# Attention with routed experts on one core: fills moved from GpSimd to VectorE, routing of two batches spread over three pairs, output transposes moved beside the products with v

## The chip, the cores and the metric

The kernel runs on one core of one Trainium2 chip. The metric is the device time of one execution in microseconds, median over the runs; lower is better. PE is TensorE (matmuls, transposes), DVE VectorE, ACT ScalarE, POOL GpSimd, SP the engine that issues most DMAs.

## The reference, cut to what matters

Inputs: q, k, v of 4 batches x 8 heads x 768 tokens x 64 values in float32, and 16 centroids per head. Every query and every key goes to the nearest centroid of its head; a query attends only to keys of its own cluster.

```python
q_assign = np.argmax(np.einsum('bhsd,hcd->bhsc', q_n, c_n), axis=-1)
k_assign = np.argmax(np.einsum('bhsd,hcd->bhsc', k_n, c_n), axis=-1)
scores = np.where(q_assign[..., None] == k_assign[..., None, :], scale * q @ k.T, -1e9)
attn = softmax(scores);  x = attn @ v                     # 3072 tokens x 512
do_compute = x @ w_skip > 0
e_idx = np.argmax(x @ w_gate, axis=1)                     # 1 of 8 experts per token
out = x;  out[do_compute] += gate_w * (relu(x @ w1[e]) @ w2[e])
```

## The kernel before, in words

**Pairs and steps.** The 32 heads are worked through as 16 pairs of heads, four pairs to a batch. A pair has 24 score steps (`score`, L654): two fp32r matmuls, L660 and L661, make a 128 x 384 tile of scores in a PSUM bank (high parts, mask rows and row maxima in L660, the low parts in L661), ACT takes the exponential (L663), GpSimd adds the tiles of a half up for the softmax sums (L669, L675). Beside the scores of one pair PE makes the row maxima of the next (`smax`, L601), each reduced by DVE (L603); L614 joins the maxima of a half, and `max_rows` (L620, L623, L628), or `mrows` (L635, L640) in pairs 0 and 1, turns them into rows of the query operand. Twice a pair, near steps 7.7 and 19.7, PE does the 12 or 24 products with v (`avs`, L686) of the half before. In the same places stand the transposes of the clusters (`assign`, L546, followed on DVE by `first_max` L526 to L539), the masks (L559), the softmax sums (L722, L734) and the output transposes (`xout`, L785, scaled by ACT in L807).

**Routing.** When the four pairs of a batch have been through, the batch is routed to the experts. `route_a` (L852) makes the logits; `route_gates` chooses the expert (L927, L934, L945) and computes the gate (`gate`: L954, L956, then g in L960, L962, L964, and its split in three bf16 parts L968 and L971, and L945 again); `route_slots` computes each token's slot: `route_c` (PE L981 to L984, DVE L988, L992, L996, L999, the one-hot rows L1003 in two pieces, L1007), `route_cum` (L1033, L1035) and `route_d` (DVE L1017 twice, PE L1022, DVE L1026). Nothing of this is wanted before the last batch is through. Then the experts run (`experts`) on the tokens that the slots list.

**Order.** A table of due times, counted in score steps, sets the order of everything up to the experts. A task of pair i with time t is due at step 24i + t; `steps` (L324) takes tasks from a heap by their due time, and every engine gets its instructions in that order. A generator yields either a delay or, in a tuple, a new due time from the start of its pair: the tables `GATES` and `SLOTS` are such times for the routing, counted from the start of the batch's last pair. So 67.66 in batch 0 (last pair 3) is step 19.66 of pair 5, and 79.66 is step 7.66 of pair 6.

**Banks.** Seven PSUM banks go round: `take` (L409) hands out the one that has been free longest, `give` (L418) puts it back. A matmul that needs a bank waits until the reader of seven takes ago has finished, so a DVE that lags stops PE. The eighth bank belongs to the products with v.

**The start.** Before pair 0 GpSimd fills operand tiles by memsets: `wraw` (L308), the two tiles MC that take the joined maxima (L312) and two rows of the query operands of pairs 1 and 2 (L315); then it does half of the low parts of pair 0 (`lo_first`, L495) and those of pair 1 (`split_lo`, L463), and `zero_rows` (L437) clears the mask rows.

Of the kernel before, what the change touches and what calls it, by code (L numbers as in the profile page):

```python
# [13 lines left out]
F32 = mybir.dt.float32  # L14
# [11 lines left out]
HP = H // 2  # L26
# [21 lines left out]
    "sims": -52.25, "assign": (-40.58, 0.23, 0.01, 0.01, 0.01, 0.01),  # L48
    "hi": (-40.33, -40.3), "masks": (-28.6, 0.12), "lo": (-28.35, -28.3), "copies": (-23.3, -23.2, -23.1),
    "smax": (-21.1, 1.0, -0.4), "mneg": (-9.0, 3.2), "mrows": ((-4.57, 0.1, 0.05), (7.4, 0.1, 0.05)),  # L50
    "av": (7.6, 13.6, 19.6), "oT": (3.5, 3.55), "sums": 43.73, "recip": 55.38, "xout": (67.43, 79.42, 37.55),
    "route": (36.0, 43.3, 58.9), "early": (85.4, 100.9),
}
OWN = {"sums": 29.2, "recip": 31.5, "xout": (31.52, 49.55, 37.55)}
ROWS = {"mrows": ((-4.5, 0.2, 0.05), (5.5, 0.1, 0.05))}

GATES = (43.31, 43.32, 43.64, 43.65, 43.66, 55.66, 55.67, 55.68, 55.69, 55.7, 55.71, 56.5,
         67.66, 67.67, 67.68, 67.69, 67.7, 67.71, 67.72, 67.73, 67.74)
SLOTS = (59.1, 60.6, 61.6, 62.6, 72.6, 74.6, 77.16, 77.17, 77.18, 77.19, 79.66, 82.9, 83.1)
FIRST = {  # L60
    0: {
        "load_v": -18.9, "sims": -20.0, "hi": (-19.9, -19.8, -19.7, -19.6), "assign": (-19.0, 0.1, 0.01, 0.01, 0.01, 0.01),
# [26 lines left out]
class Kernel:  # L89
# [202 lines left out]
    def operand_buffers(self):  # L292

        nc, fix, npair = self.nc, self.fix, self.npair
        for i in range(min(3, npair)):
            for a in range(2):
                kk = self.KB[i][a].bitcast(F32)

                lo = 64 if i else 96
                if a:  # L300
                    nc.gpsimd.memset(kk[96:98, :], 1.0)
                    nc.gpsimd.memset(kk[lo:97, :], 0.0)
                else:
                    nc.gpsimd.memset(kk[lo:98, :], 0.0)
                    nc.gpsimd.memset(kk[96:97, :], 1.0)

        self.MX = [self.mx0[:, hf * HALF:(hf + 1) * HALF].rearrange("p (b q) -> p b q", b=NB) for hf in range(2)]
        nc.gpsimd.memset(self.mx0[:, :S], 0.0)  # L308

        self.MC = [fix.tile([P, P], F32R, name=f"MC{hf}") for hf in range(2)]  # L310
        for t in self.MC:
            nc.gpsimd.memset(t.bitcast(F32), 0.0)  # L312
        for i in range(1, 3):
            for a in range(2):
                nc.gpsimd.memset(self.QM[i][a].bitcast(F32)[96:98, :], 0.0)  # L315

        self.M = [fix.tile([P, KT, 2, 3], F32, name=f"M{n}") for n in range(2)]
        for t in self.M:
            nc.vector.memset(t[:, :, :, 2:], -BIG / 2)
        nc.vector.memset(self.PT[:, :, HALF:], GUARD / S)  # L320
        for t in self.P2:
            nc.vector.memset(self.pair_of(t)[:, :, HALF:], GUARD / S)
# [24 lines left out]
    def tasks(self, i):  # L347

        p, last = dict(PLAN), i == self.npair - 1
        if not 1 < i < self.npair - 2:  # L350
            p.update(ROWS)
        if not 1 < i < self.npair - 3:
            p.update(OWN)
        elif i % HP == HP - 1:
            p["sums"], p["recip"] = 31.75, 40.0
        if i == 1:
            p["xout"] = (31.52, 55.41)
        p.update(FIRST.get(i, {}))
        r = [(s, lambda s=s: self.score(i, s)) for s in range(NS)]
        add = lambda t, f, *a: r.append((t, lambda: f(i, *a)))  # L360
        if i:
            add(p["load"], self.load)
        add(p["load_v"], self.load_v)
        if i in (1, 2):
            add(-15.0 - i * NS, self.zero_rows)
        add(p["sims"], self.sims)
        add(p["assign"][0], self.assign, *p["assign"][1:])
        if i:
            for t in range(2):
                add(p["hi"][t], self.split_hi, t)  # L370
                add(p["lo"][t], self.split_lo, t)
            add(p["copies"][0], self.copies_hi)
            for t in range(2):
                add(p["copies"][1 + t], self.copies_lo, t)
            add(p["masks"][0], self.masks, *p["masks"][1:])
        else:
            for n in range(4):
                add(p["hi"][n], self.hi_first, n % 2, n // 2)
                add(p["lo"][n], self.lo_first, n % 2, n // 2)
            add(p["masks"], self.masks_first)  # L380
        t0, dt, gap, dt2 = (*p["smax"], p["smax"][1])[:4]
        for n in range(24):
            add(t0 + dt * n if n < 12 else t0 + 12 * dt + gap + dt2 * (n - 12), self.smax, n)
        for hf in range(2):
            add(p["mneg"][hf], self.mneg, hf)
            add(p["mrows"][hf][0], self.max_rows if i > 1 else self.mrows, hf, *p["mrows"][hf][1:])
            if not 3 - hf <= i < self.npair - 2:
                for n in range(2):
                    add(12 * hf + p["av"][n], self.avs, hf, range(n * GROUP, (n + 1) * GROUP))
            else:  # L390
                add(12 * hf + p["av"][1 if hf and i == self.npair - 3 else 2], self.avs, hf, range(KT))
        if not last:
            add(p["sums"], self.sums, (0, 1))
            add(p["recip"], self.recip)
            for hf in range(2):
                add(p["xout"][2 if hf and i == self.npair - 2 else hf], self.xout, hf)
        if i == self.npair - HP - 1:
            for t, f in zip(p["early"], (self.early_lists, self.early_rows)):
                add(t, f)
        if last:  # L400
            for t, f, *a in self.ending(i):
                add(t, f, *a)
        elif i % HP == HP - 1:
            add(p["route"][0], self.route_a, i // HP)
            add(p["route"][1], self.route_gates, i // HP)
            add(p["route"][2], self.route_slots, i // HP)
        return r

    def take(self, key, shape):  # L409
# [24 lines left out]
    def zero_rows(self, i):  # L434

        for a in range(2):
            self.nc.gpsimd.memset(self.QM[i][a].bitcast(F32)[64:96, :], 0.0)  # L437

    def operands(self, i):
        c = self.st[i]  # L440
# [166 lines left out]

    def mneg(self, i, hf):

        if i:  # L610
            out = self.MC[hf][:, :2 * NB].rearrange("p (a j) -> p j a", a=2)
        else:
            out = self.MX[hf][:, :, 96:98]
        self.nc.vector.tensor_reduce(out=out, in_=self.st[i]["m"][:, hf * NB:(hf + 1) * NB], axis=AX.X, op=ALU.max)  # L614
# [247 lines left out]
    def route_gates(self, i, bt):  # L862

        nc = self.nc
        wait = iter([(t,) for t in GATES])
        lp = self.rt.tile([P, KT, H, E + 1], F32, name="lp")
        tps = []
        for hf in range(2):
            tps.append(self.take(("gs", hf), [P, NB, P]))
            for b in range(NB):  # L870
                n0 = hf * HALF + b * P
                nc.tensor.transpose(out=tps[hf][:, b, :], in_=self.rg[:, n0:n0 + P], identity=self.ident)
        for hf in range(2):
            yield next(wait)
            js = slice(hf * NB, (hf + 1) * NB)
            nc.vector.tensor_tensor(
                out=lp[:, js], in0=tps[hf].rearrange("p b (h e) -> p b h e", h=H)[:, :, :, :E + 1],
                in1=self.st[bt * HP]["rs"][:, js].unsqueeze(3).to_broadcast([P, NB, H, E + 1]), op=ALU.mult)
            self.give(("gs", hf))
        yield next(wait)  # L880
        yield from self.choose(lp, bt * KT, KT, wait)
        yield next(wait)
        yield from self.gate(i, bt * KT, KT, wait)

    def route_slots(self, i, bt):

        wait = iter([(t,) for t in SLOTS])
        yield from self.route_c(i, bt * KT, KT, wait)
        yield next(wait)
        yield from self.route_cum(KT, wait)  # L890
        yield next(wait)
        yield from self.route_d(i, bt * KT, KT, wait=wait)
# [652 lines left out]
```

## Time and profile before

| | |
|---|---|
| median of 3 runs | 655.32 us (653.06 to 657.39) |
| profiled execution | 656.28 us, of which the span of the instructions 654.4 us |
| PE busy | 630.3 us (96%) |
| DVE busy | 490.8 us (75%) |
| ACT busy | 394.6 us (60%) |
| POOL busy | 364.4 us (56%) |
| mean clock of TensorE | 0.988 of full speed |

The profiled execution is one run under the profiler; times inside it are counted in us from its first instruction. Pair 0's scores start at 20.62, pair 5 runs from 153.22 to 177.94, pair 6 to 204.60, pair 7 to 228.91, pair 9 from 256.03, pair 10 from 280.75 to 307.41; the experts begin near 436. In a row such as `[0.95 <-DVE M L603]` the bracket is the time for which the engine stood idle just before and what ended it. Matmuls overlap in the pipeline, so their starts tell more than their durations.

### The profile page before, as it was taken

What the parts mean: (1) busy time and instruction counts of PE and PEld (TensorE: products, weight loads), DVE (VectorE), ACT (ScalarE), POOL (GpSimd) and SP (SyncE); (2) the same over time, 40 slices, a digit from 0 to 9 for tenths busy, and PEclk for the clock granted to TensorE, in tenths of its full rate; (3) what the DMA queues carried; (4) which work ended last, traced back from release to release, by engine and by line L of the source; (5) the groups of instructions that cost most, each with busy time, mean ns of one, the idle gap of its engine ahead of it and who ended that gap; (6) DMA issues with size and microseconds to landing.
All of it is one profiled execution on the core that took longest, in us unless ns stands there. A gap on an engine that the chain in (4) does not pass through costs nothing.

```text
span 654.4 us, 12248 instructions
## 1 busy us (share of the span) xinstructions
PE 630.3 (96%) x3917; PEld 472.6 (72%) x3917; DVE 490.8 (75%) x1008; ACT 394.6 (60%) x907; POOL 364.4 (56%) x389
## 2 busy tenths in 40 slices
PE   7899989999999999999999999999899999999994
PEld 3576668766766777667767767646699899889783
DVE  7888587878897788988887988875869765856621
ACT  7367676666767677567766759733744645555420
POOL 9976777876778777768856867522033222211101
PEclk9799998999999999999999999999999999999998
DMA  7296666455584583674764846633386675764800
GB/s 214 78 231 161 179 166 153 145 166 131 158 221 120 146 232 97 175 179 125 202 168 132 225 108 198 210 106 113 134 261 241 209 233 195 267 204 143 275 2 33
DMA packets 54688, 110.23 MB, mean 168 GB/s; under 512 B 8783, under 2 KB 23159, under 8 KB 54624
## 3 DMA queue, kind: packets, MB, share of 16 engines
q1 hardware_dynamic: 51568, 102.01, 54.2%
q0 software_dynamic: 2656, 7.24, 3.4%
q8 instruction: 32, 0.52, 0.3%
q14 instruction: 32, 0.26, 0.1%
q10 hardware_dynamic: 400, 0.20, 0.1%
HBM read 61.00 MB, written 10.62 MB: 109 GB/s over the span
## 4 chain that ended last, share of the span: by engine, by line
PE 77%; DVE 8%; DMA 7%; issue 7%; ACT 1%; POOL 0%; SPq 0%; POOLq 0%; DVEq 0%; ACTq 0%
PE ps L686 19%; PE ps L660 10%; PE ps L601 10%; PE ps L661 9%; DVE M L603 4%; DMA out<-yo,idw 4%; PE ph L1062 3%; PE ph L1061 3%; PE ph L1060 3%; PE py L1062 2%; PE py L1060 2%; PE py L1061 2%; DMA raw<-qk 2%; PE ps L722 2%; PE ps L512 2%
## 5 line engine op out<-in xcount | busy, mean ns | idle before, releaser
L603 DVE TENSOR_REDUCE M<-ps 128x1 f32<-128x384 f32 x384 | 200.3, 554 | 60.6 <-PE ps L601 59.4
L675 POOL TENSOR_TENSOR acc<-acc,PT 128x384 f32<-128x384 f32 x134 | 126.4, 972 | 49.2 <-ACT vm L706 26.2
L660 PE MATMUL ps<-D 98*128 98x384 f32 x384 | 136.1, 355 | 1.9 <-DVE M L603 1.1
L601 PE MATMUL ps<-D 96*128 96x384 f32 x384 | 134.7, 358 | 0.8 <-ACT D L581 0.7
L675 POOL TENSOR_TENSOR acc<-acc,wraw 128x384 f32<-128x384 f32 x112 | 113.0, 1040 | 34.9 <-ACT wraw L663 34.9
L661 PE MATMUL ps<-D 128*128 128x384 f32 x384 | 131.5, 343 | 0.0
L663 ACT ACTIVATE PT<-ps 128x384 f32<-128x384 f32 x216 | 100.5, 494 | 48.5 <-PE ps L661 44.2
L663 ACT ACTIVATE wraw<-ps 128x384 f32<-128x384 f32 x168 | 81.6, 492 | 19.2 <-PE ps L661 12.6
L660 PEld LDWEIGHTS ps<-D 98*128 98x128 f32 x384 | 73.8, 192 | 20.3 <-issue 15.1
L601 PEld LDWEIGHTS ps<-D 96*128 96x128 f32 x384 | 74.3, 194 | 15.1 <-issue 6.0
L1217 POOL DMA_INDIRECT out<-yo,idw x15 | 19.3, 1287 | 116.0 <-DVE yo L1094 95.3
L686 PE MATMUL ps<-PT,vt 128*64 128x385 f32 x432 | 75.4, 492 | 0.0
L661 PEld LDWEIGHTS ps<-D 128*128 128x128 f32 x384 | 74.1, 193 | 0.0
L686 PE MATMUL ps<-wraw,vt 128*64 128x385 f32 x336 | 57.9, 492 | 0.1
L686 PEld LDWEIGHTS ps<-PT,vt 128*64 128x64 f32 x432 | 28.7, 136 | 34.8 <-issue 34.1
L1362 DVE SCALAR_TENSOR_TENSOR hl<-ph,hh 128x256 fp32r<-128x256 f32 x56 | 23.7, 423 | 38.2 <-ACT hh L1361 38.2
L1361 ACT ACTIVATE hh<-ph 128x256 fp32r<-128x256 f32 x56 | 21.5, 383 | 46.8 <-PE ph L1062 45.8
L1333 ACT ACTIVATE D<-wraw 128x1024 fp32r<-128x1024 f32 (+1 forms) x45 | 43.9, 1000 | 6.2 <-PE py L1062 6.2
L1061 PE MATMUL ph<-x2h,D 128*128 128x256 f32 x168 | 47.5, 283 | 0.0
L1060 PE MATMUL ph<-x2l,D 128*128 128x256 f32 x168 | 47.4, 283 | 0.0
L1060 PE MATMUL py<-D,hh 128*128 128x512 f32 x112 | 45.0, 402 | 0.0
L686 PEld LDWEIGHTS ps<-wraw,vt 128*64 128x64 f32 x336 | 22.7, 136 | 27.5 <-issue 26.7
(324 smaller groups left out, 1197.6 us busy)
## 6 DMA issues: line engine op xcount, KB each, us to landing
wraw<-w SPq DMA_DIRECT2D x72, 512.0 KB
D<-D SPq DMA_DIRECT2D x124, 192.0 KB
raw<-qk SPq DMA_DIRECT2D x16, 768.0 KB
D<-raw SPq DMA_DIRECT2D x60, 192.0 KB
vt<-v SPq DMA_DIRECT2D x16, 384.0 KB
out<-x SPq DMA_DIRECT2D x31, 192.0 KB
D<-mk SPq DMA_DIRECT2D x120, 24.0 KB
D<-mr SPq DMA_DIRECT2D x56, 1.5 KB
```

What stands on the lines that cost most here:

```text
L601: nc.tensor.matmul(sm, lhsT=c["qm"][a][0:96, j * P:(j + 1) * P], rhs=c["kb"][a][0:96, hf * HALF:(hf + 1) * HALF], start=True, stop=True)
L603: nc.vector.tensor_reduce(out=c["m"][:, j, a, hf:hf + 1], in_=sm, axis=AX.X, op=ALU.max)
L660: nc.tensor.matmul(ps, lhsT=c["kb"][a][0:98, ks], rhs=c["qm"][a][0:98, sl], start=True, stop=False)
L661: nc.tensor.matmul(ps, lhsT=c["kc"][a][:, ks], rhs=c["qc"][a][:, sl], start=False, stop=True)
L663: nc.scalar.activation(out=pt, in_=ps, func=AF.Exp, scale=D ** -0.5)
L675: (nc.vector if dve else nc.gpsimd).tensor_tensor(out=acc, in0=acc, in1=pt, op=ALU.add)
L686: nc.tensor.matmul(av[a * D:(a + 1) * D, :], lhsT=c["vt"][:, kt, a * D:(a + 1) * D], rhs=self.pt(i, hf * 2 * KT + kt * 2 + a), start=(kt = ...
L1060: mm(ps, lhsT=ah, rhs=bl, start=first, stop=False)
L1061: mm(ps, lhsT=ah, rhs=bh, start=False, stop=False)
L1062: mm(ps, lhsT=al, rhs=bh, start=False, stop=last)
L1333: nc.scalar.activation(out=h[:, cs], in_=r[:, cs], func=AF.Copy)
L1362: nc.vector.scalar_tensor_tensor(out=hl[:, f, :], in0=ph, scalar=0.0, in1=hh.bitcast(F32)[:, f, :], op0=ALU.max, op1=ALU.subtract)
```

## The change: fills, routing, output transposes

- **Fills.** The two memsets of MC go from GpSimd to DVE; the four of L315 go away, and `zero_rows` clears two rows more for pair 2. In pair 1 `mneg` writes the joined maxima where `mrows` reads them (`MX`); before, it wrote them to MC.
- **Routing of batches 0 and 1** (batch 2 keeps the tables; batch 3 has its own ending). The later part of the gate, from L960 on, is due at step 7.66 of pair 6 (batch 1: 10) and not at 19.66 of pair 5. The slots start at step 19.3 of pair 5 instead of 10.9, and their pieces stand at 19.66 of pair 5, 19.66 of pair 6, 7.66 and 19.3 of pair 7 (`LATE`).
- **Batch 2**: the first piece of L1003 comes from 72.6 to 67.8, the second from 74.6 to 72.6.
- **`xout`**: the output transposes of the first half from 67.43 to 67.55.

```diff
-    "av": ..., "xout": (67.43, 79.42, 37.55),
-    "route": (36.0, 43.3, 58.9), "early": (85.4, 100.9),
+    "av": ..., "xout": (67.55, 79.42, 37.55),
+    "route": (36.0, 43.3, 58.9, 67.3), "early": (85.4, 100.9),
...
-SLOTS = (59.1, 60.6, 61.6, 62.6, 72.6, 74.6, 77.16, 77.17, 77.18, 77.19, 79.66, 82.9, 83.1)
+SLOTS = (59.1, 60.6, 61.6, 62.6, 67.8, 72.6, 77.16, 77.17, 77.18, 77.19, 79.66, 82.9, 83.1)
+LATE = (79.66, 79.67, 79.68, 79.69, 79.7, 79.71, 79.72, 79.73, 79.74,
+        67.66, 67.67, 67.68, 67.69, 67.75, 91.66, 91.67, 91.68, 91.69, 103.66, 103.67, 115.3, 115.7)
...
         for t in self.MC:
-            nc.gpsimd.memset(t.bitcast(F32), 0.0)
-        for i in range(1, 3):
-            for a in range(2):
-                nc.gpsimd.memset(self.QM[i][a].bitcast(F32)[96:98, :], 0.0)
+            nc.vector.memset(t.bitcast(F32), 0.0)
...
-            add(p["route"][2], self.route_slots, i // HP)
+            add(p["route"][2 if i == self.npair - HP - 1 else 3], self.route_slots, i // HP)
...
-            self.nc.gpsimd.memset(self.QM[i][a].bitcast(F32)[64:96, :], 0.0)
+            self.nc.gpsimd.memset(self.QM[i][a].bitcast(F32)[64:96 + 2 * (i == 2), :], 0.0)
...
     def mneg(self, i, hf):
-        if i:
+        if i > 1:
             out = self.MC[hf][:, :2 * NB].rearrange("p (a j) -> p j a", a=2)
         else:
             out = self.MX[hf][:, :, 96:98]
...
     def route_gates(self, i, bt):
-        wait = iter([(t,) for t in GATES])
+        wait = iter([(t,) for t in (GATES if bt == self.nbatch - 2 else GATES[:12] + LATE[:9])])
...
     def route_slots(self, i, bt):
-        wait = iter([(t,) for t in SLOTS])
+        wait = iter([(t,) for t in (SLOTS if bt == self.nbatch - 2 else LATE[9:])])
```

From L312 on the lines of the changed kernel carry a number that is lower by one.

GpSimd's queue at the start, before (MC_205 and MC_206 are the tiles MC, D the operands):

```order
L308 MEMSET wraw 128x768
L312 MEMSET MC_205 128x128
L312 MEMSET MC_206 128x128
L315 MEMSET D 2x768 x4
L495 TENSOR_TENSOR D<-raw,D 64x768 x2
L463 TENSOR_TENSOR raw<-raw,D 128x768 x2
L437 MEMSET D 32x768 x4
L669 TENSOR_TENSOR acc<-PT 128x384 x2
```

The same place in the changed kernel:

```order
L310 MEMSET wraw 128x768
L494 TENSOR_TENSOR D<-raw,D 64x768 x2
L462 TENSOR_TENSOR raw<-raw,D 128x768 x2
L436 MEMSET D 32x768 x2
L436 MEMSET D 34x768 x2
L668 TENSOR_TENSOR acc<-PT 128x384 x2
```

Six memsets no longer stand ahead of the subtractions.

DVE's queue in pair 6, from its first row maxima to the clusters of the first products with v (M_213 and M_214 hold maxima, oht, hs, cs, cum and rhs belong to the slots of batch 0), before:

```order
L614 TENSOR_REDUCE MC_206<-M_213 128x3x2
L603 TENSOR_REDUCE M_214<-ps_88 128x1
L603 TENSOR_REDUCE M_214<-ps_91 128x1
L1007 TENSOR_TENSOR hs<-iota,hi 128x12
L1033 TENSOR_REDUCE cs<-ohd 128x8
L1035 TENSOR_TENSOR cum<-cum,cs 128x8
L1017 TENSOR_TENSOR rhs_2037<-rv,hs 128x30x8
L603 TENSOR_REDUCE M_214<-ps_89 128x1
L603 TENSOR_REDUCE M_214<-ps_94 128x1
L739 RECIPROCAL rs<-ps_92 128x3x2 x2
L526 TENSOR_REDUCE mxc<-ps_89 128x24
L1017 TENSOR_TENSOR rhs_2037<-rv,hs 128x30x8
```

The same place in the changed kernel (g and ex belong to the gate of batch 0):

```order
L602 TENSOR_REDUCE M_210<-ps_89 128x1
L602 TENSOR_REDUCE M_210<-ps_94 128x1
L602 TENSOR_REDUCE M_210<-ps_88 128x1
L602 TENSOR_REDUCE M_210<-ps_91 128x1
L738 RECIPROCAL rs<-ps_90 128x3x2 x2
L525 TENSOR_REDUCE mxc<-ps_88 128x24
L959 TENSOR_REDUCE g<-ex 128x6
L528 TENSOR_TENSOR eqc<-ps_88,mxc 128x384
L533 TENSOR_TENSOR eqc<-eqc,wts 128x384
L961 TENSOR_SCALAR g<-g 128x6
L536 TENSOR_REDUCE mwc<-eqc 128x24
L963 RECIPROCAL g<-g 128x6
```

The six pieces of the slots are gone from among the row maxima; three operations of the gate stand between the cluster operations, and six more follow them.

PE's queue at the second products of a pair (oT_103 is the attention output that is transposed), before:

```order
L785 MATMUL ps_91<-ident,oT_103 128x128 x3
L620 MATMUL ps_89<-ident_r,MC_205 128x128
L601 MATMUL ps_92<-D 128x384
L686 MATMUL ps_95<-PT,vt 64x385 x12
L512 MATMUL ps_88<-raw,cb_184 32x384 x2
```

In the changed kernel:

```order
L619 MATMUL ps_91<-ident_r,MC_205 128x128
L600 MATMUL ps_89<-D 128x384
L784 MATMUL ps_92<-ident,oT_103 128x128 x3
L685 MATMUL ps_95<-PT,vt 64x385 x12
L511 MATMUL ps_88<-raw,cb_184 32x384 x2
```

The three transposes move behind the maxima rows and one row-maximum matmul, right ahead of the products. This happens in ten pairs, 2 to 11.

## Rows read from the trace of the kernel before

**Rows 1.** Page, part 4: shares of the chain of work that ended last.

```profile
PE 77%; DVE 8%; DMA 7%; issue 7%; ACT 1%; POOL 0%; SPq 0%; POOLq 0%; DVEq 0%; ACTq 0%
```

**Rows 2.** Busy time by stretch (pairs 2, 6, 10): length, PE, PEld, DVE, ACT, POOL, clock, DMA.

```profile
75.14:102.50 27.36, 25.55 (x144) 18.65 (x145) 20.12 (x40) 18.09 (x47) 20.61 (x22) 0.95 0.58 152
...
177.94:204.60 26.66, 25.31 (x161) 17.86 (x161) 22.91 (x45) 17.79 (x47) 20.29 (x21) 1.00 0.59 156
...
280.75:307.41 26.66, 25.32 (x160) 17.87 (x160) 22.90 (x45) 17.79 (x47) 20.29 (x21) 1.00 0.59 156
```

**Rows 3.** Timeline, PE, 160 to 192: start, duration, operation, idle before.

```profile
163.29 0.34 PE L601 MATMUL ps<-D 96*128 96x384 f32 x1
...
163.46 0.34 PE L660 MATMUL ps<-D 98*128 98x384 f32 x1
...
167.22 0.33 PE L601 MATMUL ps<-D 96*128 96x384 f32 x1
...
167.81 0.44 PE L660 MATMUL ps<-D 98*128 98x384 f32 x1 [0.25 <-DVE M L603]
...
181.95 0.45 PE L660 MATMUL ps<-D 98*128 98x384 f32 x1 [0.34 <-DVE M L603]
...
183.34 0.52 PE L785 MATMUL ps<-ident,oT 128*128 128x128 f32 x3
...
184.80 0.55 PE L546 MATMUL ps<-ident,ss 128*128 128x128 f32 x3 [0.95 <-DVE M L603]
```

**Rows 4.** Timeline, DVE, 160 to 191.

```profile
166.05 0.19 DVE L992 TENSOR_REDUCE rank<-rk 128x6 f32<-128x48 f32 x1
...
166.62 0.68 DVE L996 TENSOR_SCALAR hi<-rank 128x6 f32<-128x6 f32 x1
...
171.94 0.74 DVE L962 TENSOR_SCALAR g<-g 128x6 f32<-128x6 f32 x1
...
175.10 0.31 DVE L945 TENSOR_TENSOR rv<-vals,ohd 128x144 bf16<-128x144 bf16 x1
...
176.55 2.68 DVE L603 TENSOR_REDUCE M<-ps 128x1 f32<-128x384 f32 x5 [1.14 <-PE ps L601]
...
185.86 1.20 DVE L1017 TENSOR_TENSOR rhs<-rv,hs 128x240 bf16<-128x240 bf16 x1
```

**Rows 5.** Timeline, DVE and POOL, around the first products of pair 7.

```profile
212.64 0.66 DVE L539 TENSOR_TENSOR oh<-wts,mwc 128x384 bf16<-128x384 f32 x1
...
214.33 2.15 DVE L603 TENSOR_REDUCE M<-ps 128x1 f32<-128x384 f32 x4 [1.03 <-PE ps L601]
...
215.67 3.63 POOL L675 TENSOR_TENSOR acc<-acc,PT 128x384 f32<-128x384 f32 x4 [2.78 <-ACT vm L706]
```

**Rows 6.** Timeline, POOL, at the start.

```profile
13.28 2.77 POOL L315 MEMSET D<- 2x768 f32 x4
...
19.90 3.91 POOL L463 TENSOR_TENSOR raw<-raw,D 128x768 fp32r<-128x768 f32 x2
```

**Rows 7.** Timeline, DVE and PE, at the start.

```profile
22.75 1.47 DVE L539 TENSOR_TENSOR oh<-wts,mwc 128x384 bf16<-128x384 f32 x1
...
22.63 0.52 PE L661 MATMUL ps<-D 128*128 128x384 f32 x1
...
24.28 0.50 PE L559 MATMUL ps<-ident_bf,oh 128*128 128x128 bf16 x3 [1.13 <-DVE oh L539]
```

**Rows 8.** Busy time by stretch, at the start (columns as in Rows 2).

```profile
20.00:25.00 5.00, 3.30 (x13) 2.67 (x13) 4.90 (x6) 2.52 (x6) 4.94 (x4) 0.62 0.46 162
...
25.00:30.00 5.00, 5.00 (x25) 4.06 (x25) 3.28 (x8) 2.46 (x5) 4.92 (x7) 0.70 0.11 26
```

**Rows 9.** Timeline, PE, in pair 2.

```profile
98.24 0.85 PE L512 MATMUL ps<-raw,cb 128*32 128x384 f32 x8 [1.81 <-DMA raw<-qk]
```

**Rows 10.** Timeline, PE and DVE, in pair 1.

```profile
56.63 0.49 PE L635 MATMUL ps<-ident,wraw 128*128 128x128 f32 x3
...
56.74 0.17 DVE L614 TENSOR_REDUCE MC<-M 128x6 fp32r<-128x18 f32 x1
```

More of the change, by code (lines that the diff above doesn't have):

```diff
@@ L50 @@
     "smax": (-21.1, 1.0, -0.4), "mneg": (-9.0, 3.2), "mrows": ((-4.57, 0.1, 0.05), (7.4, 0.1, 0.05)),
-    "av": (7.6, 13.6, 19.6), "oT": (3.5, 3.55), "sums": 43.73, "recip": 55.38, "xout": (67.43, 79.42, 37.55),
-    "route": (36.0, 43.3, 58.9), "early": (85.4, 100.9),
+    "av": (7.6, 13.6, 19.6), "oT": (3.5, 3.55), "sums": 43.73, "recip": 55.38, "xout": (67.55, 79.42, 37.55),
+    "route": (36.0, 43.3, 58.9, 67.3), "early": (85.4, 100.9),
 }
```

## The prediction, as put on record

> **What bounds the kernel now.** I read the chain of waits first: PE is 77% of it [rows 1]. Then the busy times pair by pair, with the pairs' first scores as limits, to see where PE is not busy. Pairs 6 and 10, the second pairs after the last of a batch, last 26.66 us each with PE busy for 25.31 and 25.32 [rows 2], so 1.35 us each is idle. Both carry the same routing steps, for batch 0 and batch 1, and show the same numbers. Everything else between the start and the experts is PE with no gap to speak of, except the start and pair 2. So I looked in PE's timeline for what ends the idle time [rows 3], in DVE's for what stood in DVE's queue there [rows 4], and at the start [rows 6 to 8]. The change does not touch the experts, about a third of the span.
>
> The stalls in pairs 5 and 6 work like this. Seven PSUM banks go round, and a lagging DVE returns the bank of a row maximum late; PE then waits for L603. At 167.81 PE waited 0.25 us, at 181.95 0.34, at 184.80 0.95 [rows 3], 1.54 in all. Each restart also costs: the first matmul behind a wait lasts 0.44 to 0.55 instead of 0.34. From start to start, L601 to L660 takes 0.17 in the ordinary case (163.29 to 163.46) and 0.59 at 167.22 to 167.81, so this stall is worth 0.42 and not 0.25. I add 0.16 to each: 0.42 + 0.50 + 1.11 = **2.0 us per batch**, 4.0 for two.
>
> How much lag is free? Ahead of 167.81, L992 (0.19), a multiply of the same size and L996 (0.68) had been put in among the maxima [rows 4], about 1.07 us; PE lost 0.42. So about **0.65 us** of lag costs PE nothing, an estimate.
>
> **The change, part by part.**
>
> *Routing out of the maxima.* The six slot pieces no longer stand among the row maxima of pairs 5 and 6; they come next to products with v, where DVE has no maxima to make. I take off the whole 2.0 per batch. The pieces and the gate need cover in their new places:
> - Pair 5, second products: L988 to L999 and a piece of L1003 take the place of the nine gate operations. Those ran from 171.94 (L962) to 175.41 (end of L945), and DVE still idled 1.14 us before the next maximum at 176.55 [rows 4]. The new ones are fewer. Cost nothing; without the cover, about as much as was taken off.
> - Pair 6, second products: the other piece of L1003 and L1007 to L1035. The same cover, not otherwise used. Nothing.
> - Pair 6, first products: the nine gate operations, behind and among the cluster operations. The cover is to be read in pair 7, which has no routing there: L539 starts at 212.64, lasts 0.66, and the next maximum comes at 214.33 after 1.03 us idle [rows 5]. Upper bound: the gate as it ran beside GpSimd's adds, 175.41 − 171.94 less one L463 that ran in between and plus L960, about 2.8 us; 2.8 − 1.03 − 0.65 = 1.1 us of stall. Lower bound: nine operations of 0.2, the price of L992 or L945 at 0.19 to 0.31, 1.9 us: 1.9 − 1.03 − 0.65 = 0.2. I take 0.25, near the lower end, because in pair 7 GpSimd has done its adds by then: it idled 2.78 us before 215.67 [rows 5], so from 212.9, and the last six operations run without it.
> - Pair 7, first products: L1017 twice. One took 1.20 beside the adds [rows 4]: 2.4 − 1.03 − 0.65 = 0.75 at most, 0 at least. I take 0.1: the gap is half filled at the least price and one of the two can be expected to be short.
>
> Left over per batch 0.35 (0 to 1.85). PE's own routing matmuls only move. **Routing: −4.0 + 0.7 = −3.3 us** (−4.0 to −0.3).
>
> *Fills.* GpSimd's four memsets of L315 take 2.77 us from 13.28 on; then come L495 and L463 (19.90, for 3.91) [rows 6]. DVE's L539 at 22.75, beside L463, took 1.47 us, against 0.66 in pair 7 [rows 5, 7]; L534 before it was held up alike. PE came to L559 after the L661 of 22.63, which is over in 0.52 with its successor due after 0.32, and started at 24.28: 1.33 us lost, 1.13 of it named as waiting for L539 [rows 7]. With 2.77 us less ahead of it, L463 ends near 21 and L539 is done before PE asks. All of the 1.33 goes. DVE's two new memsets lie in its idle time before the first clusters: nothing; without that cover, two at the price of L992, 0.4.
>
> What the 1.33 is worth depends on the clock. TensorE ran at a mean granted clock of 0.62 from 20 to 25 and 0.70 from 25 to 30, though busy throughout the second stretch [rows 8]: half of these ten us was at the lower of the two levels, 1.2 GHz, and 0.38 × 5 + 0.30 × 5 = 3.4 us of full-speed work was lost. Pair 2 shows what one spell of waiting costs: after the 1.81 us at 98.24 [rows 9] the clock of the pair is 0.95 of 27.36 us [rows 2], 1.4 lost. The start has two idle spells, before the first score and at L559. If the low clock lasts as long as now, only about 0.6 of the 1.33 is kept, 0.8. If the second spell is what prolongs it, up to half of the 3.4 is added: 0.8 + 1.7 = 2.5. I take **−1.9**, above the middle, since two spells cost over twice what one did.
>
> *Maxima of pair 1.* L635 at 56.63 now waits for L614, which starts at 56.74 and ends at 56.91 [rows 10]: **+0.3** (0 to 0.3). Behind the wait on PE stand the maxima and scores; they come that much later. In the first half L614 is done long before.
>
> *Batch 2.* One piece of L1003 moves to just ahead of maxima that follow the products without pause. Its nearest price is L1017's 1.20; less 0.65, at most 0.5. It leaves an equal lag later. **+0.2** (0 to 0.5).
>
> *Output transposes.* The same PE instructions in another order, ten times. L785's three lie between matmuls either way; a pitch may be 0.05 longer or shorter. **0** (−0.5 to +0.5). ACT's and SP's order is unchanged; the maxima rows leave PE a little sooner, for which nobody waits.
>
> **Sum:** −3.3 − 1.9 + 0.3 + 0.2 = −4.7. The profiled execution took 656.28, its span plus 1.9; that gives 651.6. It stands 1.0 above the median of the runs shown, so against the median it would be 650.6. I forecast **651.0 us**.
>
> **A rule that speaks against the new places.** Operations of the same size cost very different times here: L962 on 128 x 6 elements took 0.74, L992, which reads eight times as much, 0.19 [rows 4]. The Trainium skill ("SBUF — State Buffer", section "Who interferes with whom") says that DVE and GpSimd share a port pair, that a copy, cast or tensor_scalar in a two-port mode contends for it and that whoever came first blocks the other for its whole instruction, while a tensor_reduce never contends. By that rule a gate operation amid the adds would wait out what is left of an add. The two rows agree with it. By the rule alone all four tensor_scalar and cast operations of the gate would be long in pair 6, and the time would be that of the second rival.
>
> **Rivals.**
> 1. *The clock stays low as long as now.* The start gives 0.8 instead of 1.9: 652.1. For it: the first idle spell stays. Chance 0.2.
> 2. *The gate waits behind GpSimd's adds again.* Four operations at 0.74 and two long L1017: the left-over is 1.85 per batch and not 0.35, so 651.0 + 3.0 = 654.0. For it: rows 4; against: GpSimd idles by the end of the clusters [rows 5]. Chance 0.15.
> 3. *Slower.* The stall moves into one place, the first maximum after the gate in pairs 6 and 10, and grows to what waiting cost in pair 2. If the gate's 2.8 us meets both adds and cluster operations that are each lengthened as L539 was at the start (by 0.8), the lag is 2.8 + 0.8 − 1.03 = 2.6, the stall 1.9: that is the length that preceded a low clock at 98.24, and another 1.4 us go. Per batch 3.3 against 2.0 taken off, plus pair 7's 0.75: +2.05, so +4.1 in all, and with the start −1.9 and +0.5: 656.3 + 2.7 = 659.0. It decides from a stall of 1.8 us; rows 5 speak against. Chance 0.04.
> 4. *Better.* Nothing is left over, the start gives 2.5 and the low clock in pair 2 is spared by another timing of that wait: 651.0 − 0.7 − 0.6 − 1.4 = 648.3. Chance 0.15.
>
> That the slots come too late cannot be: L1026 of batch 1 is due in pair 11, far ahead of the experts.
>
> **How the numbers follow.** The forecast's own case has 0.46. The range **647 to 655** takes in the forecast, rivals 1, 2 and 4 and the bounds of the sum on either side but for the extremes together. 1% is 6.55 us, about what can be told from no change: 648.8 to 661.9. Faster by over 1%: rival 4 and the lower edge of the forecast, 0.17. Slower by over 1%: 0.02, the worse half of rival 3. Within: the rest, 0.81.
>
> **What would show it.** Pairs 6 and 10 should last about 25 us, with PE idle 0.5 at most; PE should no longer wait for L603 ahead of L546. L495 should start near 13.5, L559 near 23, and the clock from 25 to 30 be above 0.70. L635 in pair 1 should be released by L614. I am wrong if the gate's operations in pair 6 hold back the next row maximum by over 1.7 us, if pair 5 stalls anew, or if the start is no shorter.

## The result, and the profile after

| | before | changed |
|---|---|---|
| median | 655.09 us (653.06 to 657.39, 4 runs) | 647.89 us (647.10 to 649.57, 4 runs) |
| ratio, 95% interval | | 0.9882 (0.9861 to 0.9902) |
| profiled execution | 656.28 us, span 654.4 | 649.57 us, span 647.7 |

The change makes the kernel 1.2% faster, 7.2 us between the medians and 6.7 between the two profiled executions. The forecast was 651.0, range 647 to 655. I lay out the spans of the two profiles by pairs, from first score to first score; the columns are those of [rows 2].

| stretch | before | changed | difference |
|---|---|---|---|
| start, to the first score | 20.62 | 20.95 | +0.33 |
| pair 0 | 28.25 | 27.46 | -0.79 |
| pair 1 | 26.26 | 26.51 | +0.25 |
| pair 2 | 27.36 | 25.02 | -2.34 |
| pairs 3 and 4 | 50.72 | 50.89 | +0.17 |
| pairs 5, 6, 7 | 75.69 | 73.47 | -2.22 |
| pair 8 | 27.12 | 27.17 | +0.05 |
| pairs 9, 10, 11 | 75.69 | 73.48 | -2.21 |
| pairs 12 to 15 | 104.07 | 104.19 | +0.12 |
| experts to the end | 218.60 | 218.58 | -0.02 |

Busy time of the changed kernel in pairs 0, 2, 6 and 10:

```profile
20.95:48.41 27.46, 26.34 (x138) 20.05 (x138) 21.57 (x40) 16.35 (x35) 20.75 (x24) 0.88 0.63 150
74.91:99.93 25.02, 24.10 (x145) 17.21 (x145) 19.98 (x40) 18.13 (x47) 18.78 (x21) 1.00 0.64 167
...
174.99:199.71 24.72, 24.72 (x154) 17.92 (x154) 23.02 (x50) 17.77 (x47) 18.27 (x21) 1.00 0.62 168
...
275.64:300.37 24.73, 24.73 (x155) 17.93 (x155) 22.72 (x50) 17.76 (x47) 19.31 (x21) 1.00 0.62 167
```

The 0.33 by which the first score comes later is not the fills': in the eight other kernels with the same memsets (below) it comes at 20.62 to 20.69.

Pairs 6 and 10 are now wholly PE: length and busy time are equal, where 1.35 us was idle [rows 2]. Where PE waited 0.95 us ahead of L546 [rows 3], PE's timeline now shows

```profile
179.45 0.52 PE L784 MATMUL ps<-ident,oT 128*128 128x128 f32 x3
179.80 0.49 PE L545 MATMUL ps<-ident,ss 128*128 128x128 f32 x3
```

0.35 us from start to start instead of 1.46. DVE's timeline at the gate's new place in pair 6 and at the two L1016 in pair 7 (L1017 before):

```profile
182.32 0.97 DVE L961 TENSOR_SCALAR g<-g 128x6 f32<-128x6 f32 x1
...
183.78 0.56 DVE L538 TENSOR_TENSOR oh<-wts,mwc 128x384 bf16<-128x384 f32 x1
184.26 0.17 DVE L967 CAST vals<-g 128x6 bf16<-128x6 f32 x1
...
185.29 0.31 DVE L944 TENSOR_TENSOR rv<-vals,ohd 128x144 bf16<-128x144 bf16 x1
185.51 1.94 DVE L602 TENSOR_REDUCE M<-ps 128x1 f32<-128x384 f32 x4
...
205.52 0.64 DVE L1016 TENSOR_TENSOR rhs<-rv,hs 128x240 bf16<-128x240 bf16 x1
...
207.23 1.20 DVE L1016 TENSOR_TENSOR rhs<-rv,hs 128x240 bf16<-128x240 bf16 x1
...
209.45 2.15 DVE L602 TENSOR_REDUCE M<-ps 128x1 f32<-128x384 f32 x4
```

One gate operation among the clusters was held up (L961, 0.97); the six behind L538 took their short times, as [rows 5] let one expect once GpSimd's adds are through. The next maxima follow without idle time, so the cover of 1.03 us is used up. DVE is then late by a little more than PE can take. PE's timeline names no wait behind these products, but its starts show three delays:

```profile
186.12 0.44 PE L659 MATMUL ps<-D 98*128 98x384 f32 x1
186.40 0.34 PE L660 MATMUL ps<-D 128*128 128x384 f32 x1
...
188.17 0.34 PE L600 MATMUL ps<-D 96*128 96x384 f32 x1
188.50 0.45 PE L659 MATMUL ps<-D 98*128 98x384 f32 x1
188.78 0.34 PE L660 MATMUL ps<-D 128*128 128x384 f32 x1
```

From start to start these take 0.28, 0.33 and 0.28 us where 0.18 is usual, 0.35 in all, and all of it counts as busy. The run with the gate left where it was (below) does not have them.

At the start, POOL, DVE and PE:

```profile
13.84 3.71 POOL L494 TENSOR_TENSOR D<-raw,D 64x768 fp32r<-64x768 f32 x2 [0.93 <-DVE D L494]
17.63 3.58 POOL L462 TENSOR_TENSOR raw<-raw,D 128x768 fp32r<-128x768 f32 x2
...
22.25 0.56 DVE L538 TENSOR_TENSOR oh<-wts,mwc 128x384 bf16<-128x384 f32 x1
...
23.35 0.52 PE L660 MATMUL ps<-D 128*128 128x384 f32 x1
23.68 0.54 PE L558 MATMUL ps<-ident_bf,oh 128*128 128x128 bf16 x3
```

L462 ends at 21.2 and not at 23.8 [rows 6], L538 takes 0.56 and not 1.47 [rows 7], and L558 starts 0.33 behind the matmul ahead of it: the wait is gone. The clock is not:

```profile
20.00:25.00 5.00, 4.43 (x17) 3.88 (x17) 4.00 (x8) 2.90 (x6) 4.42 (x6) 0.58 0.18 73
25.00:30.00 5.00, 5.00 (x25) 3.99 (x25) 3.29 (x8) 2.55 (x6) 3.14 (x4) 0.74 0.13 30
```

0.42 × 5 + 0.26 × 5 = 3.4 us of full-speed work is lost, as before [rows 8]. In pair 2 the wait for the load is shorter than in [rows 9], 0.92 us, and the clock stays at 1.00:

```profile
96.93 0.85 PE L511 MATMUL ps<-raw,cb 128*32 128x384 f32 x8 [0.92 <-DMA raw<-qk]
```

In pair 1 PE waits for the maxima, but for 0.2 us only (columns: total, times, longest):

```profile
PE ps L634 <- DVE wraw L613: 0.2, 1, 0.2
```

### The profile page after: what moved, and what is told of

Same layout as the page of the kernel before. It is cut to its first block, busy times and chain, and to the rows that moved or that the text cites. A ratio compares the mean times of both kernels' runs of the same rounds, so it can differ in the third digit from the quotient of the medians.

```text
span 647.7 us, 12258 instructions
## 1 busy us (share of the span) xinstructions
PE 629.3 (97%) x3917; PEld 473.2 (73%) x3917; DVE 493.6 (76%) x1010; ACT 394.4 (61%) x907; POOL 356.0 (55%) x383
## 4 chain that ended last, share of the span: by engine, by line
PE 81%; issue 7%; DMA 6%; DVE 4%; ACT 1%; POOL 0%; POOLq 0%; SPq 0%; DVEq 0%; ACTq 0%
PE ps L685 19%; PE ps L659 11%; PE ps L600 11%; PE ps L660 10%; DMA out<-yo,idw 4%; PE ph L1060 3%; PE ph L1059 3%; PE ph L1061 3%; PE py L1061 2%; PE py L1059 2%; PE py L1060 2%; PE ps L511 2%; PE ps L721 2%; PE ps L784 2%; DVE M L602 2%
## 5 line engine op out<-in xcount | busy, mean ns | idle before, releaser
L602 DVE TENSOR_REDUCE M<-ps 128x1 f32<-128x384 f32 x384 | 199.0, 553 | 49.9 <-PE ps L600 48.6
L674 POOL TENSOR_TENSOR acc<-acc,wraw 128x384 f32<-128x384 f32 x112 | 109.1, 1006 | 38.3 <-ACT wraw L662 38.3
L662 ACT ACTIVATE wraw<-ps 128x384 f32<-128x384 f32 x168 | 81.7, 492 | 17.8 <-PE ps L660 10.9
```

The lines of the kernel that those rows point to most:

```text
L602: nc.vector.tensor_reduce(out=c["m"][:, j, a, hf:hf + 1], in_=sm, axis=AX.X, op=ALU.max)
L662: nc.scalar.activation(out=pt, in_=ps, func=AF.Exp, scale=D ** -0.5)
L674: (nc.vector if dve else nc.gpsimd).tensor_tensor(out=acc, in0=acc, in1=pt, op=ALU.add)
```

## The experiments

Each kernel was timed beside the kernel before on the same chip, and the ratios refer to that. The medians of the kernel before were 655.56 us beside the routing, the fills, the transposes and the load, 654.88 beside the dummy matmuls, the doses, the memsets and the gate, and 656.36 beside the other three.

### The parts alone

**Routing alone.** The routing's lines of the diff in the kernel before (`LATE`, the fourth entry of `route`, and the two iterators).

> The kernel before with the routing of batches 0 and 1 spread as in the change, and nothing else. Theory: the stalls behind L603 vanish without anything in their place; pairs 5 to 7 and 9 to 11 together are 2.2 us shorter per batch, 4.4 in all, ratio about 0.993; pair 0 stays at 28.2. Rival: part of the 4.4 came from an earlier start or the moved output transposes, then it is under 3.5. Pair 2: if its 2.3 us in the change came with the routing (it cannot by the order, since no routing operation stands there), it is 25.0 here, else 27.4.

650.55 us, ratio 0.9924 (0.9898 to 0.9949), that is −5.0 us (−6.7 to −3.3). Pairs 5 to 7 last 73.34 and 9 to 11 73.35 us, −4.7 together; pair 6 lasts 24.68, as in the change. Pairs 0 and 2:

```profile
20.66:47.19 26.53, 23.54 (x138) 17.27 (x138) 22.81 (x40) 16.24 (x35) 23.44 (x25) 1.00 0.69 182
73.53:100.70 27.17, 25.55 (x145) 18.64 (x145) 20.03 (x39) 17.99 (x47) 20.49 (x22) 0.95 0.59 154
...
PE ps L561 <- DVE oh L541: 1.9, 1, 1.9
```

The whole of the routing gain is here. Something else shows: pair 0, untouched by this edit, was 1.7 us shorter than in the profile before, because the clock did not fall at the start of this run, and its wait for the clusters (L561 here) was then 1.9 us long, not 1.1.

**Fills alone.** The fills' lines of the diff in the kernel before, with `mneg`.

> The kernel before with the fills alone (MC on DVE, four memsets dropped, two rows more in zero_rows, the maxima of pair 1 in MX). Theory: L559 no longer waits for L539, but TensorE's clock is as low for as long as before, so that pair 0 is 0.8 us shorter, pair 1 0.25 longer, total -0.5, ratio 0.999. Rival: the fills also shorten pair 2 by 2.3 us, because the load that it waits for comes earlier against PE; then the total is -2.9, ratio 0.9955.

652.67 us, ratio 0.9954 (0.9937 to 0.9971): −3.0 us (−4.1 to −1.9).

```profile
20.64:44.70 24.06, 23.51 (x138) 17.25 (x138) 20.40 (x40) 16.25 (x35) 19.81 (x23) 1.00 0.62 153
71.32:96.53 25.21, 24.32 (x146) 17.32 (x145) 19.86 (x40) 18.06 (x46) 18.64 (x20) 1.00 0.64 165
```

At full clock pair 0 goes from 26.53 (above) to 24.06, −2.5 us, three times the −0.8 that the two profiles at the lower clock show. Not all of that is the fills'. The wait at the clusters goes from 1.9 to 0.2, which is 1.7: L559 starts at 24.25 to 24.33 in all four kernels with the old memsets, whenever PE gets there, and at 22.5 to 22.6 in all with the new ones and the clock up. The other 0.8 is a second wait, late in the pair, for L603: 1.1 us before and in the routing alone, 0.3 here. With these memsets and the clock up, pair 0 lasts 24.0 to 24.8 in six other kernels, and in the three longer ones that second wait is 1.1 as before. So the fills are worth 1.7 to 2.5 us of pair 0 at full clock, and what sets the second wait stays open.

Over the runs the clock gains too. The mean clock of the nine runs here and the ten of the memsets alone (below) is 0.994, against 0.991 in the 35 runs of the kernel before beside them. It falls less often with these memsets, whether at the start or in pair 2 the profiles are too few to say. A line through the runs of the kernel before gives 0.4 us for each 0.001 of mean clock, so by this estimate some 1.2 of the 3.0 us come by the clock. Pair 2 is short here too, and the total is the rival's, so the rival seemed right until the memsets were run alone (below).

**Output transposes alone.** `"xout"` 67.43 to 67.55.

> The kernel before with the output transposes of the first half moved, nothing else. Theory: within 0.5 us of before; pairs 4, 8 and 12 longer by 0.05 each. Rival: the move is what shortens pair 2, whose maxima rows leave PE and SP sooner: then pair 2 is 25.0 instead of 27.4, ratio 0.9965.

657.28 us, ratio 1.0012 (0.9992 to 1.0032): no difference that can be told. By the order of PE's matmuls the ten pairs with a move are 4 to 13, not 2 to 11 as the section on the change has it. Pairs 4 to 12 are 0.03 to 0.11 us longer here, 0.5 together; pair 13 is 0.74 longer, with a wait of 0.6 us for ACT that no other kernel has there. Pair 2 lasted 26.04 with the wait for the load at 1.7 us. The clock stayed at 1.00 in that pair, though it had fallen in pair 0 (0.88, 29.30 us), where PE waited 1.9 us at L559.

**The memsets without the maxima of pair 1.** As the fills, but `mneg` as before.

> The kernel before with the memsets of the change (MC on DVE, L315 dropped, two rows more in zero_rows), and the maxima of pair 1 left in MC. Theory: the wait in pair 2 for q and k of pair 5 goes from 1.7 to 0.9 us because of the memsets (fewer GpSimd instructions move the code fetches against the loads): pair 2 is 25.2 here; pair 1 is 26.26, 0.3 shorter than with the fills whole. Rival: it comes from the 0.3 us by which pair 1 got longer: then pair 2 stays at 26 to 27.4.

651.91 us, ratio 0.9954 (0.9935 to 0.9973). Pair 0 lasted 24.05, pair 2 28.06, longer than in any other kernel, with a wait of 2.2 us: so the memsets do not shorten that wait, and the theory falls. So does its rival: with pair 1 made longer by `mneg` alone (next) the wait is 1.9 us. Over the eleven profiles of kernels with the load in its old order the wait was 0.9 twice (the changed kernel, the fills) and 1.5 to 2.2 us in the other nine, with the memsets and without. The last packets of the load end 20.9 to 22.9 us after the pair's start, though it is issued at 15.0 to 15.2 in all. In several of the late ones the last packets come 0.23 us apart, as if one of the 16 DMA engines were behind; the cause was not settled.

**Maxima of pair 1 alone.** The one line of `mneg` in the kernel before.

> The kernel before with the joined maxima of pair 1 written where mrows reads them, and nothing else. Theory: L635 waits for L614 and pair 1 is 0.2 to 0.3 us longer than its 26.3. Rival: the 0.3 by which pair 1 is longer in all kernels with the memsets of the change comes from these alone, and pair 1 stays at 26.3.

One run, 653.74 us. L635 waits 0.2 us for L614; pair 1 lasts 26.66, 0.40 longer than before. It also lasts 26.62 with the memsets alone, where L635 does not wait. That run lost the time at another place, at the first score of pair 2, for the transfer of the maxima rows (`mr`):

```profile
PE ps L657 <- DMA D<-mr: 0.4, 1, 0.4
```

Without this wait its pair 1 is 26.24, as before. So the 0.2 to 0.4 of pair 1 come with the line of `mneg`; the memsets add none.

### What DVE's lag costs PE

**Dummy reductions among the maxima** of the changed kernel:

```diff
+        for i, n in ((3, 2), (4, 4), (7, 6), (8, 8), (11, 10), (12, 12)):
+            tasks.append((i * NS + 2.6, 0, lambda n=n: [self.nc.vector.tensor_reduce(
+                out=spare, in_=self.ident, axis=AX.X, op=ALU.max) for _ in range(n)] and None))
```

> The changed kernel with dummy reductions on DVE (128x128 to 128x1, result unused) put among the row maxima at step 2.6 of pairs 3, 4, 7, 8, 11 and 12: 2, 4, 6, 8, 10 and 12 of them, at about 0.2 us each. Theory: a lag of 0.65 us is free and what is above it costs PE one for one: the pairs are longer by 0, 0.15, 0.55, 0.95, 1.35, 1.75. Rival: the cost starts at once (0.4 to 2.4), or the products with v take it up and nothing under 2 us is lost.

One run, 657.61 us. Six of them, in DVE's timeline of pair 7, and PE's waits for L606 (L602 in the changed kernel) in all:

```profile
200.70 1.88 DVE L331 TENSOR_REDUCE spare<-ident 128x1 f32<-128x128 f32 x6
202.50 0.55 DVE L606 TENSOR_REDUCE M<-ps 128x1 f32<-128x384 f32 x1
...
PE ps L663 <- DVE M L606: 7.2, 5, 2.7
```

202.50 − 200.70 = 1.80 for six, so 0.30 each and not the 0.2 expected. Against the changed kernel, in us:

| pair | put in | lost | put in − lost |
|---|---|---|---|
| 4 | 1.2 | 0.41 | 0.79 |
| 7 | 1.8 | 1.08 | 0.72 |
| 8 | 2.4 | 1.69 | 0.71 |
| 11 | 3.0 | 2.35 | 0.65 |
| 12 | 3.6 | 2.97 | 0.63 |

Pair 3, with 0.6, lost nothing. A lag of about 0.7 us is free, and beyond it PE loses as much as DVE is given, as the theory had it. The clock stayed at 1.00 in these pairs, though PE waited 2.7 us at a stretch.

**The gate left where it was.** `GATES` in place of `GATES[:12] + LATE[:9]` in the changed kernel.

> The changed kernel with the later part of the gate of batches 0 and 1 left where it was, at step 19.66 of pair 5 and 9, beside the new slot pieces. Theory: gate (2.8 us) and pieces (about 2.4) together are longer than the cover there (2.8 + 1.1 idle + 0.65 free), so that PE loses about 0.7 us in pairs 5 and 9 and nothing elsewhere: +1.4 against the changed kernel. Rival: the cover is longer than read and nothing is lost.

647.64 us, ratio 0.9890 (0.9860 to 0.9919), which cannot be told from the change. My theory is wrong: nothing is lost in pairs 5 and 9 (24.17 and 24.18), and pairs 6 and 10 are 0.36 shorter, 24.37:

```profile
173.34:197.71 24.37, 24.37 (x154) 18.03 (x154) 21.85 (x41) 17.77 (x47) 18.30 (x21) 1.00 0.63 170
```

So the gate's new place costs 0.36 us in each of pairs 6 and 10: these are the three delays in PE's starts shown above. DVE's timeline at the second products of pair 5, where gate and slots now stand together:

```profile
166.85 0.19 DVE L959 TENSOR_REDUCE g<-ex 128x6 f32<-128x48 f32 x1
...
167.08 0.60 DVE L961 TENSOR_SCALAR g<-g 128x6 f32<-128x6 f32 x1
...
168.55 0.17 DVE L967 CAST vals<-g 128x6 bf16<-128x6 f32 x1
...
171.28 0.55 DVE L1002 TENSOR_TENSOR oht<-iota,los 128x384 bf16<-128x384 f32 x1
171.95 3.74 DVE L602 TENSOR_REDUCE M<-ps 128x1 f32<-128x384 f32 x7
```

From 166.85 to 171.83 it all fits, to 0.1 us: while one operation waits for GpSimd's add the rest behind it comes out short, and the last piece (L1002), which took 1.2 us beside an add in the changed kernel, takes 0.55 once the adds are through. I had added up prices that do not occur together.

**Four kinds of tiny operations among the maxima** of the changed kernel, four times each, in pairs 7, 8, 11 and 12:

```diff
+        for i, kind in zip((7, 8, 11, 12), kinds):
+            for s in (2.6, 3.6, 4.6, 5.6):
+                tasks.append((i * NS + s, 0, lambda kind=kind: kind() and None))
```

> The changed kernel with four tiny DVE operations (result unused) among the row maxima of each of pairs 7, 8, 11 and 12, at steps 2.6, 3.6, 4.6 and 5.6, of one kind in each pair: reductions of 128x48 to 128x6, tensor_scalar on 128x6, casts of 128x6, subtractions of two tiles 128x6, all beside GpSimd's adds. Theory: only kinds that share a port with GpSimd wait: reductions 0.19 each, the other three between 0.2 and 1.0 as the adds happen to stand, 0.6 in the mean; PE loses nothing in pair 7 and up to 0.8 in the others. Rival: size alone or the place decides, all four cost 0.2.

One run, 655.40 us. Durations of the four (least, median, most, in ns), in order of the pairs 7, 8, 11, 12:

```profile
L332 DVE TENSOR_REDUCE spare<-iota x4: 193/194/195, 201.3 to 203.1; 128x6 f32<-128x48 f32 x4
L333 DVE TENSOR_SCALAR spare<-iota x4: 233/398/442, 225.8 to 228.1; 128x6 f32<-128x6 f32 x4
...
L334 DVE CAST sparb<-iota x4: 252/402/441, 303.9 to 306.1; 128x6 bf16<-128x6 f32 x4
...
L335 DVE TENSOR_TENSOR spare<-iota x4: 243/390/431, 328.7 to 330.9; 128x6 f32<-128x6 f32 x4
```

The reductions read eight times as much and cost half as much; the other kinds vary as the adds stand. Each kind had a pair of its own here, so the pair could be the cause; the doses above rule that out, since their 42 reductions took the same time in all six pairs:

```profile
L331 DVE TENSOR_REDUCE spare<-ident x42: 274/286/288, 101.0 to 334.6; 128x1 f32<-128x128 f32 x42
```

That the kind decides is shown. It is what the Trainium skill says ("SBUF — State Buffer", section "Who interferes with whom"): tensor_reduce never contends with GpSimd; a tensor_scalar, a cast and a tensor_tensor with two inputs in SBUF can. PE lost 0.2 us in pairs 8, 11 and 12, and nothing in pair 7.

The time was lost elsewhere, in pairs without any of the new operations: 1.9 us in pair 1, 1.1 in pair 2, 0.7 in pair 5, 1.7 in pair 9, 2.0 in pair 13 and 1.7 in pair 14 against the changed kernel. Pair 1 waits 0.65 and 1.05 us for transfers, and pair 2 1.8 for the load; pair 14 ran at a granted clock of 0.94, behind a wait of 1.8 us for DVE at its first score. DVE and POOL in pair 9:

```profile
256.98 2.52 DVE L543 TENSOR_TENSOR eqe<-eqe,wts 128x48 f32<-128x48 f32 x1
...
255.84 3.60 POOL L684 TENSOR_TENSOR acc<-acc,PT 128x384 f32<-128x384 f32 x4
```

A multiply of 128x48 that takes 0.70 us in the changed kernel at the same place took 2.52, until the fourth of four adds ended (255.84 + 3.60 = 259.44). The same happened in pairs 5 and 13, 2.52 each time. Here the measurement goes past the Trainium skill, which has the loser blocked for the other's whole instruction ("SBUF — State Buffer", section "Who interferes with whom"): it was blocked for more than one. Nor is it this run's alone. Single subtractions of 128x768 (L463 before, 0.95 us at other places) took 2.9 to 3.8 us at places in twelve of the thirteen profiles, the one before included, where a row of adds stood beside them; in the changed kernel, DVE and POOL:

```profile
192.28 3.45 DVE L462 TENSOR_TENSOR raw<-raw,D 128x768 fp32r<-128x768 f32 x1
...
191.31 3.61 POOL L674 TENSOR_TENSOR acc<-acc,wraw 128x384 f32<-128x384 f32 x4
```

What tips it is open.

### The start and the load of pair 5

**Dummy matmuls in PE's idle spells at the start** of the changed kernel:

```diff
-        tasks += [... for t, n in ((-20.05, 2), (-19.05, 2), (-18.0, 7))]
+        tasks += [... for t, n in ((-20.05, 2), (-19.05, 2), (-18.0, 7), (-12.81, 4), (-12.75, 2))]
```

> The changed kernel with six more dummy matmuls (128x512 bf16 into the spare bank, no result used) at the start: four between the transposes L545 and L634, where PE stood idle 1.2 us, two between L634 and the first score, where it stood idle 0.6 us. Theory: those spells are what lets TensorE's clock fall at the first scores; filled, the clock stays at full speed, pair 0 lasts 24.1 us as in the run of the fills alone and not 27.5, the same in every run, so the median falls by the share of runs that now lose it (1 to 2.5 us, about 646.5). Rival: the fall comes from elsewhere (idle before 13 us, the load of the array at half rows), then pair 0 is between 24 and 27.5 as before and the median is 647.9.

647.07 us, ratio 0.9877 (0.9856 to 0.9899), which lies between theory and rival and cannot be told from the change's 0.9882.

```profile
20.00:25.00 5.00, 4.65 (x29) 3.46 (x30) 4.90 (x10) 3.98 (x9) 4.86 (x7) 1.00 0.14 52
```

The clock stayed up, and pair 0 lasted 24.83 us. But the clock also stayed up without the dummies in seven profiles (the routing, the fills, the memsets, the maxima of pair 1, the gate, the doses, the four kinds), and fell at the start in four: before, the change, the transposes and the load below. With the dummies (here and in the last kernel) the mean clock of eleven runs was 0.993 to 0.997, against 0.990 to 0.997 of the change's four. It looks as if they help; the change's own runs are too few to show it.

**The load of pair 5 first.** `5: {"load": -64.1}` among the tables of the changed kernel.

> The changed kernel with one load moved: q and k of pair 5 are issued ahead of v of pair 4, in pair 2. Theory: the 0.9 us for which PE waits at the clusters of pair 5 for that load goes, pair 2 lasts 24.1 instead of 25.0, total -0.9 against the changed kernel, and the clock does not fall in pair 2. Rival: v of pair 4 comes too late and PE waits for it at its first products, or the load is bound by the transfers ahead of it and the wait stays.

648.27 us, ratio 0.9880 (0.9854 to 0.9905), not better than the change as far as can be told. The wait for the load is gone, but PE now waits for DVE in the same pair (pair 2 25.35 us):

```profile
PE ps L660 <- DVE M L603: 0.8, 1, 0.8
```

Neither theory expected that. A reading that was not tested: the wait for the load had given DVE time to catch up. What is gained is that the pair no longer depends on how late the load comes.

**What the runs point to.** The dummies, the load first, the gate left where it was, the output transposes back at 67.43.

> The changed kernel with what the runs so far point to: six dummy matmuls in PE's idle spells at the start, q and k of pair 5 loaded ahead of v of pair 4, the gate of batches 0 and 1 left at step 19.66, the output transposes back where they were. Theory: the start keeps its clock (pair 0 24.1 to 24.8), pair 2 lasts 25.3 whatever the transfers do, pairs 6 and 10 are 0.36 shorter, ten pairs 0.05 shorter each: about 645 us against 647.9 for the change. Rival: these only move waits, the load's to L603 and the clock's fall to pair 2, and the median stays within 0.1% of the kernel with the dummy matmuls alone, 647.1.

645.75 us (644.92 to 646.24), ratio 0.9838 (0.9819 to 0.9857): 2.1 us under the change's median, on another chip, their intervals against before just apart; from the dummy matmuls alone (0.9856 to 0.9899) it can hardly be told. By the pairs the theory held, but for pair 14, which is 0.5 us longer than in the change. Pairs 0, 2 and 6:

```profile
20.66:45.50 24.84, 23.50 (x138) 17.24 (x138) 21.18 (x40) 16.24 (x35) 20.58 (x24) 1.00 0.65 160
72.02:97.30 25.28, 24.47 (x145) 17.27 (x145) 20.46 (x41) 18.67 (x48) 18.84 (x21) 1.00 0.62 165
172.16:196.59 24.43, 24.43 (x155) 18.07 (x154) 21.89 (x42) 17.60 (x47) 18.51 (x21) 1.00 0.63 170
```

Its five runs lie within 1.3 us, where the nine of the kernel before beside them spread over 3.1: that fits a spread that comes for the most part from the clock and the load.

## Why the prediction was right, and where not

The direction, the mechanism of the main term and the range held. The size was too small: −4.7 in the sum, −7.2 measured. That put the median 0.9 us above the range's lower edge, near rival 4's 648.3, and under the 648.8 to which I had given 0.17. About 1 us of the gain comes by the clock: at the same mean clock, by the line of 0.4 us for each 0.001 (an estimate), the change's four runs are 6.4 us faster than before. By the steps:

- **Routing out of the maxima**, −3.3 forecast, −4.4 in the two profiles, −5.0 (−6.7 to −3.3) timed alone. The mis-sized term is the stalls: 2.0 per batch in the sum, 2.6 in the runs (pairs 5 to 7 take 75.69 us before and 73.13 with the gate left where it was). I had counted three restarts and left a fourth out, which no wait names:

```profile
180.41 0.34 PE L601 MATMUL ps<-D 96*128 96x384 f32 x1
180.81 0.44 PE L660 MATMUL ps<-D 98*128 98x384 f32 x1
```

That is 0.40 from start to start where 0.17 is usual. Behind a restart the next matmul, too, starts 0.1 later than usual (0.28 where 0.18 is usual), which I had not added. The left-over came out as forecast in all, 0.36 per batch against 0.35, but only for the gate, forecast at 0.25; the two L1016 in pair 7, forecast at 0.1, cost PE nothing: pair 7 is 0.26 longer than before by the six slot matmuls that moved there and the transposes. The free lag of 0.65 was right (0.7 by the doses), and so was the place where the gate's tail runs clear of the adds.
- **Fills**, −1.9 forecast, −0.8 between the profiles, −3.0 (−4.1 to −1.9) timed with `mneg` and without. The mis-sized term is the wait, because I priced it from a run at the lower clock, in which PE reached L559 later and so waited less: 1.1 us there, 1.9 in the run of the routing alone, at full clock. At full clock pair 0 gains 1.7 to 2.5. My second part, a clock that is low for a shorter time, did not come in the changed kernel's profile: there rival 1 came true to the digit (0.8), with 3.4 us lost as before. Over the runs it came in another form, as a clock that falls less often (0.994 against 0.991). One reading was wrong: 3.4 us lost means that two thirds of the ten us were at the lower level, not half.
- **Maxima of pair 1**, +0.3 forecast; 0.2 of wait, and pair 1 0.2 to 0.4 longer.
- **Batch 2**, +0.2 forecast; nothing was measured. Pair 13 is 0.06 longer in the change, but with the output transposes back where they were and batch 2 as in the change (the last kernel above) it is as before.
- **Output transposes**, 0 (±0.5) forecast; 0.05 per pair, the upper end.
- **Pair 2** was in no term; only rival 4 had it. The 2.3 us between the profiles are not shown to be the change's: kernels with the same memsets had pair 2 between 25.0 and 28.1. The timed parts add up without it, −5.0 − 3.0 + 0.8 = −7.2, where the change's own ratio gives −7.7 (−9.1 to −6.4); with 1.1 to 1.7 us of doubt on each part that is agreement and no proof.
- **Rival 2** (the gate waits behind the adds) did not come: of its four operations one did. **Rival 3** (slower) had its price right in kind: the doses show one for one loss past 0.7, and the held multiply shows that one operation can take 2.5 us. But its last step is not certain: the clock fell behind the wait of 1.8 us for DVE in the run of the four kinds and did not behind one of 2.7 among the doses. **Rival 4** (better) had the time nearly right, but not its conditions: something was left over, and pair 2 kept its clock in the changed kernel's profile by a shorter wait that only the profile of the fills repeats.

## What to carry to other kernels

Small operations that are not urgent cost nothing beside a stretch in which their engine has no work that PE waits for, as long as the stretch and the slack behind it cover them, and all of their length beyond the slack beside work that PE does wait for; the slack can be measured with doses. An engine that a view shows as wholly busy can still be held up: compare the starts of its instructions with those of an undisturbed pair. A price read from one profile holds for that run's clock: look at the spread of the runs, and ask what in it is the clock, before a pair's difference is put down to an edit. Prices of operations that wait for a neighbour do not add up, since while one waits the neighbour gets done.

## What the runs showed of the hardware that was not expected

- Whether TensorE's clock falls at the start differs from profile to profile (it fell in four of eleven profiles without the dummy matmuls); it cost 3.4 us of full-speed work in three of them and 1.7 in the fourth, the load first. The Trainium skill ("TensorE: Matmul & The Clock Gate", Part 1) says that the number of slow matmuls at a kernel's start varies between runs of the same kernel. The runs agree in kind: the mean clock of the kernel before was 0.987 to 0.997 in 44 of them. A fall in pair 2 came behind waits of 1.6 to 2.2 us in four kernels and did not behind 1.5 to 2.1 in five others.
- A load issued at the same moment of the pair landed up to 1.9 us apart.
- A DVE operation with two inputs in SBUF can take as long as a whole row of GpSimd's adds beside it: 2.5 us for one that takes 0.2 elsewhere, 2.9 to 3.8 for one that takes 0.95.
